# Sparse attention and an MLP on one core: regrouping the TensorE runs of batch 1, and two products less in batch 0

## The chip, the core and the metric

The kernel runs on one core of a Trainium2 chip. The metric is the device time of one execution in microseconds. A core has TensorE (PE in the profile, with its weight loads as PEld), VectorE (DVE), ScalarE (ACT), GpSimd (POOL) and SyncE (SP, used here to issue DMAs). TensorE writes to PSUM; DVE and ACT read PSUM and write SBUF.

## The reference, cut to what matters

```
B, H, S, D = 8, 8, 576, 64
scores = q @ k^T / sqrt(D)
local mask   (heads 0-3): 0 <= i - j < 32
strided mask (heads 4-7): i >= j and j % 32 == i % 32
attn = softmax(where(mask, scores, -1e9)) @ v          # per head
x    = attn, heads side by side                        # 4608 tokens x 512
h    = x @ w_in                                        # 512 -> 2048
g    = h * tanh(softplus(h))                           # Mish
out  = g @ w_out                                       # 2048 -> 512
```

## The kernel before, in words

Only the scores that a mask lets through are computed. The local heads are cut into 6 tiles of 96 queries, two head pairs each (12 units); the strided heads into 16 units of 72 queries. Each kind has three parts: the strided kind's parts 0, 1 and 2 hold 6, 6 and 4 units, the local kind's 5, 5 and 2. The third parts are what the change calls the third scores.

An attention step is one of these, all written out in program order by hand (`tc.manual_schedule()`), so that each engine's order is the order of the code:

- `t_str` and `t_loc` transpose q or k by PE into a PSUM tile. A call is for one pair of heads (`hp`); `t_loc` makes 12 transposes of 96 columns and returns the eviction, which the caller gives to DVE or ACT. `qTl` and `kTl` are the results for the local heads.
- `qk` (short `Q`) computes the scores of one or more parts in one run of matmuls (line 310), and ACT's exponentials (line 320 or 324) follow, one for each part.
- `mask` (`M`) multiplies by the mask on DVE (line 330).
- `pv` (`V`) multiplies the probabilities by v for one tile of queries (4 matmuls, line 346) into a small PSUM tile, and DVE normalises: a reciprocal (357) and a multiplication (358). `pv2` does two neighbouring tiles into one accumulator, with one reciprocal (371) and one multiplication (372) for both.
- `xt` and `xt_now` (`X`) transpose the result for the MLP; `xt_later` does so by DMA.

PSUM has small tiles of one bank, `tile_t`, of which two exist and are handed out in turn, and accumulators of two banks, `acc(0)` to `acc(2)`. A new use of a tile waits until what the last use left in it has been read.

The MLP goes by blocks of 512 tokens. While block t is computed, the attention of batch t+1 is threaded in. Block 0 differs from the others: its second product (`mlp2`, line 802) has 16 groups of four 512-column matmuls, and after group i the steps `at[i]` of batch 1 are issued. Their list is returned by `attn_steps` in the case `x == y`, where the one accumulator that attention has is `acc(x)`, with x = 0. The other blocks use another list, which the change leaves as it is. Some loads and sums of the weights hang on the same step numbers: `sums_w` on steps 0, 7, 9 and 11, loads for batch 2 on step 3 (issued by POOL), the transposing DMAs of batch 2 on step 12 (issued by SP), `sums_x` on step 14.

Batch 0 is computed ahead of the blocks, with nothing beside it. Between its steps stand products of a tile of zeros that nothing reads, `unread(n, i_acc)` (line 258): n matmuls of 512 columns into a small tile or into the first half of an accumulator. The call at line 931 is `unread(2, 2)`, between the transposes of the strided q (lines 929 and 930) and the bias matmuls of the third strided part (line 932), which write the same accumulator.

Of the kernel before, what the change touches and what calls it, by code (L numbers as in the profile page):

```python
# [11 lines left out]
BF16 = mybir.dt.bfloat16  # L12
# [31 lines left out]
def kernel(ctx, tc, q, k, v, moe_w_in, moe_w_out, out):  # L44
    nc = tc.nc
# [60 lines left out]
    def acc(i, name):  # L106

        pool = ps_z[0] if i == 2 else ps_a
        return pool.tile([128, 2, 512], F32, tag=f"acc{i}", name=name)
# [10 lines left out]
    def tile_t(name):  # L120
        return ps_t.tile([128, 512], F32, tag="pt", name=name)
# [11 lines left out]
    def by_head(x):  # L133

        return x[0:PL].rearrange("p j h d -> p (j h d)").rearrange("p (h x) -> p h x", h=4)
# [19 lines left out]
    def spread_v_str(b, eng):  # L155
        cast(eng, vs[b % 2][0:PN, :, :, 0:D], vs_raw().rearrange("p h (j d) -> p h j d", d=D))
# [23 lines left out]
    def cast(eng, out_, in_):  # L180
        if eng is nc.scalar:
            nc.scalar.copy(out_, in_)  # L182
        else:
            eng.tensor_copy(out_, in_)
# [35 lines left out]
    def t_loc(b, which, hp, tr):  # L220
        src = by_head((ql if which == "q" else kl)[b % 2])
        for j in range(CL):
            for e in range(2):
                nc.tensor.transpose(
                    tr[64 * e:64 * e + 64, PL * j:PL * j + PL],
                    src[:, 2 * hp + e, D * j:D * j + D], ident[0:PL, 0:PL],
                )
        dst = qTl[:, hp, :] if which == "q" else kTl[:, hp, 32:32 + S]
        return lambda eng: cast(
            eng, dst.rearrange("c (p j) -> c p j", j=CL),  # L230
            tr[:, 0:S].rearrange("c (j p) -> c p j", j=CL),
        )

    def t_str(b, which, hp, tr):
        src = (qs if which == "q" else ks)[b % 2]
        for u in range(8):
            h, jj = 2 * hp + u // 4, u % 4
            nc.tensor.transpose(  # L238
                tr[:, PN * u:PN * u + PN], src[0:PN, h, 128 * jj:128 * jj + 128],
                ident[0:PN, 0:PN],  # L240
            )
        dst = (qTs if which == "q" else kTs)[:, 8 * SU * hp:8 * SU * hp + 8 * SU]
        return lambda eng: cast(
            eng, dst.rearrange("c (u n) -> c u n", u=8)[:, :, 0:PN],
            tr[:, 0:S].rearrange("c (u n) -> c u n", u=8),
        )

    def t_step(b, kind, which, hp, eng=None):

        eng = eng or nc.vector  # L250
        tr = tile_t("tr")[:].bitcast(BF16)
        (t_str if kind == "s" else t_loc)(b, which, hp, tr)(eng)

    def unread(n, i_acc=None):

        tr = tile_t("un")[:] if i_acc is None else acc(i_acc, "un")[:, 0, :]
        for _ in range(n):
            nc.tensor.matmul(tr, lhsT=zeros[:, 0:128], rhs=zeros, start=True, stop=True)  # L258
# [165 lines left out]
    def attn_steps(b, x, y):  # L424

        a = Attn(b)
        Q = lambda i_acc, *parts: (lambda: a.qk(parts, i_acc))
        M = lambda kd, i: (lambda: a.mask(kd, i, nc.vector))
        V = lambda kd, i: (lambda: a.pv(kd, i))
        X = lambda kd, hf: (lambda: a.xt(kd, hf))  # L430
        s0, s1, sl2, l0, l1 = ("s", 0), ("s", 1), (("s", 2), ("l", 2)), ("l", 0), ("l", 1)
        if x == y:
            T = [(lambda n=n: t_step(b, *T_ORDER[n])) for n in (2, 3)]

            def t_first():
                tr = acc(x, "tr")
                copies = [t_str(b, w, 0, tr[:, n, :].bitcast(BF16)) for n, w in enumerate("kq")]
                for copy in copies:
                    copy(nc.vector)

            def t_pair(which):
                tr = acc(x, "tr")
                copies = [t_loc(b, which, hp, tr[:, hp, :].bitcast(BF16)) for hp in range(2)]
                for copy, eng in zip(copies, (nc.vector, nc.scalar)):
                    copy(eng)

            return [
                T,
                [Q(x, s0), Q("t", s1), lambda: spread_v_str(b, nc.vector), M(*s0), M(*s1)],
                [],  # L450
                [V("s", 0)],
                [V("s", 1), Q(x, ("s", 2))],
                [V("s", 2), M("s", 2), lambda: t_pair("k")],
                [V("s", 3)],
                [V("s", 4), lambda: t_pair("q")],
                [V("s", 5)],
                [V("s", 6), Q(x, l0)],
                [V("s", 7), M(*l0), Q(x, l1)],
                [X("s", 0), V("l", 0), M(*l1), Q(x, ("l", 2))],
                [X("s", 1), V("l", 1), M("l", 2)],  # L460
                [V("l", 2), V("l", 3)],
                [V("l", 4), V("l", 5)],
                [lambda: a.xt_now(5, nc.vector), lambda: a.xt_later(5)],
            ], [t_first]
        V2 = lambda kd, i, z: (lambda: a.pv2(kd, i, z))
        G = lambda kd, i: (lambda: a.mask(kd, i, nc.gpsimd))
        l2 = ("l", 2)
        now = -(-(512 * (b + 1) - S * b) // WQ)
        at = [
            [],  # L470
            [Q(x, s0), Q(y, s1), Q("t", *sl2), M(*s0), M(*s1), M("s", 2)],
            [],
            [V2("s", 0, y), G(*l2)],
            [],
            [V2("s", 2, y), Q(x, l0), Q("t", l1), G(*l0), G(*l1)],
            [],
            [V2("s", 4, y), lambda: nc.scalar.preload_act_table(AF.Mish)],
            [],
            [V2("s", 6, y)],
            [V2("l", 0, x)],  # L480
            [X("s", 0), V2("l", 2, y), X("s", 1)],
            [V2("l", 4, x), lambda: a.xt_now(now)],
            [lambda: a.xt_later(now)],
        ]
        return at
# [395 lines left out]
    with tc.manual_schedule():  # L881
# [39 lines left out]
        a = Attn(0)  # L921
# [6 lines left out]
        unread(5, 2)  # L928
        t_step(0, "s", "q", 0, Sc)
        t_step(0, "s", "q", 1, Dv)  # L930
        unread(2, 2)
        ps.append(a.bias("s", 2, 2))
        for i in range(2):
            a.qk([("s", i)], None, ps[i])
# [44 lines left out]
        for t in range(NBLK):  # L979
            if t == 0:  # L980
                x, y, z = accs
                at, ts = attn_steps(1, y, y)
                at[3] += [
                    lambda: load_early_v_str(2), lambda: load_tiles_loc(2, kl, k, (0, 1)),
# [13 lines left out]
            else:  # L998
                if t == 1:
                    split_third()  # L1000
                x, y = 0, 1
                gT, z, g1 = mlp1(t, (y, x) if t == 1 else (x, y))
                at = attn_steps(t + 1, x, y) if t + 1 < B else []
                if t == 1:
                    at[0].append(lambda: sums_w()[3](hi))
# [63 lines left out]
```

## Time and profile before

| | us |
|---|---|
| median of 3 runs (lowest, highest) | 285.5 (285.01, 285.75) |
| the profiled execution | 285.73 |
| its span on the core | 284.0 |
| PE busy | 277.0 |
| DVE busy | 199.1 |
| ACT busy | 197.3 |
| POOL busy | 109.6 |

The span runs from the first to the last instruction; the 1.7 us beside it in the execution's time lie around it. Busy times are sums over the span and can overlap between engines. Batch 0's attention fills about the first 22 us, the first product of block 0 the time to 34 us, the second product with the steps of batch 1 the stretch from 34 to 56 us; from there on one block follows another.

### The profile page before, as it was taken

How to read it: one execution, taken by the hardware profiler on the slowest of the kernel's cores; microseconds unless marked ns; L12 is line 12 of the kernel's file. 1: busy time of each engine (PE TensorE's matmuls, PEld its weight loads, DVE VectorE, ACT ScalarE, POOL GpSimd, SP SyncE). 2: the span in 40 equal slices, each digit the busy share in tenths (PEclk: the TensorE clock that was granted, in tenths of full speed). 3: DMA queues.
4: the chain of work that ended last, by engine and by line, in shares of the span. 5: the costliest groups of instructions: out<-in, count | busy, mean ns of one | idle time of the engine just before them, and what ended most of it. 6: DMA issues, size and time to landing. Idle time of an engine off the chain costs nothing.

```text
span 284.0 us, 7580 instructions
## 1 busy us (share of the span) xinstructions
PE 277.0 (98%) x3128; PEld 220.7 (78%) x3143; DVE 199.1 (70%) x415; ACT 197.3 (69%) x296; POOL 109.6 (39%) x129
## 2 busy tenths in 40 slices
PE   8999999999999999999999999999999999999994
PEld 2565755686898689868988898789878997888683
DVE  4176778889786778778767778777877767644742
ACT  1578663699857985798679877987798769417820
POOL 8584457307380729071907173625432500000000
PEclk9999999999999999999999999999999999999999
DMA  8999999999997999699969998999979041003004
GB/s 148 186 206 203 190 168 165 145 175 220 147 159 126 219 174 163 113 217 156 174 115 214 158 151 140 212 129 179 131 210 71 3 162 24 0 30 120 2 0 148
DMA packets 102685, 40.14 MB, mean 141 GB/s; under 512 B 85116, under 2 KB 98156, under 8 KB 102652
## 3 DMA queue, kind: packets, MB, share of 16 engines
q0 software_dynamic: 37728, 15.12, 50.6%
q1 hardware_dynamic: 64636, 24.31, 48.7%
q8 instruction: 24, 0.39, 0.6%
q10 hardware_dynamic: 288, 0.25, 0.3%
q14 instruction: 9, 0.07, 0.1%
HBM read 36.82 MB, written 9.44 MB: 163 GB/s over the span
## 4 chain that ended last, share of the span: by engine, by line
PE 86%; DMA 7%; DVE 2%; ACT 2%; SPq 1%; issue 1%; POOL 0%; DVEq 0%; POOLq 0%
PE pso L769 26%; PE psu L535 10%; PE psb L535 9%; PE psv L535 8%; PE psh L512 7%; DMA ql<-in_q_dram 6%; PE pso L829 4%; PE psb L512 4%; PE pso L802 4%; PE po L346 4%; PE un L258 3%; PE ps L310 3%; DMA kTl<-kl 1%; PE trx L395 1%; PE tr L238 1%; ACT Pl L324 1%
## 5 line engine op out<-in xcount | busy, mean ns | idle before, releaser
L535 PEld LDWEIGHTS <-w_in 128*128 128x128 bf16 x416 | 40.5, 98 | 9.2 <-issue 0.3
L769 PEld LDWEIGHTS <-gT 128*128 128x128 bf16 x448 | 41.9, 98 | 5.8
L330 POOL TENSOR_TENSOR Pl<-Pl,consts_sb 128x960 bf16<-128x960 bf16 (+1 forms) x18 | 29.2, 1636 | 43.3 <-issue 30.2
L769 PE MATMUL pso<-w_out,gT 128*128 128x256 bf16 x336 | 40.9, 272 | 0.0
L769 PEld LDWEIGHTS <-Sg 128*128 128x128 bf16 x336 | 31.5, 98 | 4.4
L535 PEld LDWEIGHTS <-Sw 128*128 128x128 bf16 x312 | 30.5, 98 | 4.0
L182 ACT COPY xT<-trx 128x576 bf16<-128x576 bf16 (+3 forms) x24 | 14.2, 629 | 18.5 <-PE trx L395 12.8
L512 PEld LDWEIGHTS <-w_in 128*128 128x128 bf16 x176 | 17.1, 98 | 12.6 <-issue 0.5
L769 PE MATMUL pso<-Tw,Sg 128*128 128x256 bf16 x224 | 26.7, 273 | 0.0
L544 ACT ACTIVATE gT<-psu 128x1024 bf16<-128x1024 f32 x18 | 18.5, 1025 | 9.9 <-PE psu L535 9.9
L160 POOL DMA_DIRECT2D vl<-in_v_dram x30 | 22.6, 760 | 6.9 <-DMA w_out<-in_moe_w_out_dram 2.6
L182 ACT COPY osb<-pso 128x512 f32<-128x512 f32 (+1 forms) x17 | 9.4, 555 | 20.2 <-PE pso L769 10.8
L512 PE MATMUL psh<-xT,w_in 128*128 128x512 bf16 (+1 forms) x95 | 22.2, 361 | 0.6
L675 DVE TENSOR_TENSOR psu<-psb,p 128x512 f32<-128x512 f32 x18 | 12.6, 700 | 14.5 <-PE psb L535 13.5
L372 DVE TENSOR_TENSOR x_s<-po,rden 72x512 bf16<-72x512 f32 x28 | 19.2, 687 | 1.0
L535 PE MATMUL psb<-Sx,w_in 128*128 128x256 bf16 x144 | 19.4, 272 | 0.0
L535 PE MATMUL psu<-xT,w_in 128*128 128x256 bf16 x136 | 18.9, 272 | 0.2 <-ACT psb L560 0.2
L675 DVE TENSOR_TENSOR Sg<-gT 128x256 bf16<-128x256 bf16 (+2 forms) x32 | 12.8, 422 | 8.0 <-ACT gT L544 6.7
L647 POOL COPY mark<-qTl 1x4 bf16<-1x4 bf16 x6 | 2.0, 334 | 42.4 <-DMA qTl<-ql 34.1
L746 DVE TENSOR_TENSOR p<-pso,p 128x512 f32<-128x512 f32 x14 | 9.6, 685 | 11.8 <-PE pso L769 11.8
L512 PE MATMUL psb<-xT,w_in 128*128 128x512 bf16 (+1 forms) x72 | 16.4, 355 | 0.0
L802 PE MATMUL pso<-w_out,gT 128*128 128x512 bf16 x59 | 15.8, 380 | 0.4 <-issue 0.2
(141 smaller groups left out, 617.5 us busy)
## 6 DMA issues: line engine op xcount, KB each, us to landing
out_dram<-osb SPq DMA_DIRECT2D x9, 512.0 KB, 3.9
out_dram<-p SPq DMA_DIRECT2D x7, 512.0 KB, 3.0
kl<-in_k_dram SPq DMA_DIRECT2D x5, 576.0 KB, 13.8
ql<-in_q_dram SPq DMA_DIRECT2D x5, 576.0 KB, 16.3
qs<-in_q_dram POOLq DMA_DIRECT2D x8, 288.0 KB, 12.3
vsr<-in_v_dram POOLq DMA_DIRECT2D x8, 288.0 KB, 9.8
vl<-in_v_dram POOLq DMA_DIRECT2D x30, 72.0 KB, 4.8
w_in<-in_moe_w_in_dram POOLq DMA_DIRECT2D x4, 512.0 KB, 12.1
```

The lines of the kernel that those rows point to most:

```text
L160: nc.gpsimd.dma_start(vl[b % 2][32:128, :, h, 0:D], v[b, h].rearrange("(w p) d -> p w d", p=WQ))
L182: nc.scalar.copy(out_, in_)
L330: meng.tensor_tensor(out=pm, in0=pm, in1=mk[0:n, :].unsqueeze(1).unsqueeze(1).to_broadcast([n, 2, nu, w]), op=ALU.mult,)
L346: nc.tensor.matmul(po[:, h, :], lhsT=pt[0:n, c0:c0 + 128], rhs=rhs, start=True, stop=True,)
L372: nc.vector.tensor_tensor(out=dst.rearrange("p e (h d) -> p e h d", h=4), in0=po[0:m, :, :, 0:D], in1=rden[0:m].unsqueeze(3).to_broadcast( ...
L512: nc.tensor.matmul(ps_u[:, o:o + n], lhsT=w_in[:, cc, fc * 128:(fc + 1) * 128], rhs=xT[:, cc, a:a + n], start=(cc == 2 and (o == 0 or len( ...
L535: nc.tensor.matmul(p[:, 256 * j:256 * j + 256], lhsT=lhs[:, cc, f:f + 128], rhs=rhs[:, cc], start=(first and j == 0 and cc == 0), stop=(la ...
L544: nc.scalar.activation(gT[:, c:c + src.shape[1], 256 * half_t:256 * half_t + 256], src, AF.Mish,)
L675: nc.vector.tensor_tensor(out=out_, in0=in0, in1=in1, op=op)
L769: nc.tensor.matmul(ps[:, pair, :], lhsT=lhs(c, 128 * pair), rhs=rhs(c), start=(first and pair == 0 and c == 0), stop=(last and c == 7), sk ...
L802: nc.tensor.matmul(p[:, ot % 2, :], lhsT=gT[:, fc, 128 * ot:128 * ot + 128], rhs=w_out[:, fc, :], start=(fc == 0), stop=(fc == 15),)
L829: nc.tensor.matmul(ps[n][:, 0:256], lhsT=lhs(c, 128 * n), rhs=rhs(c), start=(first and c == 0), stop=(last and c == 7), skip_group_check=True,
```

## The change: what it does

In the list of batch 1's steps:

- The local q and k, which were transposed in two runs of 24 (k in step 5, q in step 7, both into the accumulator), are transposed in one run of 48 in step 5: q into the two small tiles, k into the accumulator. ACT evicts the first half of q and of k, DVE the second halves.
- The third strided scores (step 4) and the third local scores (step 11) are computed in one run in step 7, with the two exponentials behind it. The strided mask that follows goes from step 5 to step 8; the local one stays in step 12.
- The strided products 1 and 2 (steps 4 and 5) become one `pv2` in step 4, the local products 2 and 3 (step 13) one `pv2` in the same step, both in the accumulator.

In batch 0 the call `unread(2, 2)` goes.

```diff
-            def t_pair(which):
+            def t_local():
+                copies = [t_loc(b, "q", hp, tile_t("tr")[:].bitcast(BF16)) for hp in range(2)]
                 tr = acc(x, "tr")
-                copies = [t_loc(b, which, hp, tr[:, hp, :].bitcast(BF16)) for hp in range(2)]
-                for copy, eng in zip(copies, (nc.vector, nc.scalar)):
+                copies += [t_loc(b, "k", hp, tr[:, hp, :].bitcast(BF16)) for hp in range(2)]
+                for copy, eng in zip(copies, (nc.scalar, nc.vector) * 2):
                     copy(eng)
 
             return [
...
                 [V("s", 0)],
-                [V("s", 1), Q(x, ("s", 2))],
-                [V("s", 2), M("s", 2), lambda: t_pair("k")],
+                [lambda: a.pv2("s", 1, x)],
+                [t_local],
                 [V("s", 3)],
-                [V("s", 4), lambda: t_pair("q")],
-                [V("s", 5)],
+                [V("s", 4), Q(x, *sl2)],
+                [M("s", 2), V("s", 5)],
                 [V("s", 6), Q(x, l0)],
                 [V("s", 7), M(*l0), Q(x, l1)],
-                [X("s", 0), V("l", 0), M(*l1), Q(x, ("l", 2))],
+                [X("s", 0), V("l", 0), M(*l1)],
                 [X("s", 1), V("l", 1), M("l", 2)],
-                [V("l", 2), V("l", 3)],
+                [lambda: a.pv2("l", 2, x)],
                 [V("l", 4), V("l", 5)],
...
         t_step(0, "s", "q", 1, Dv)
-        unread(2, 2)
         ps.append(a.bias("s", 2, 2))
```

## The prediction

> **What bounds the kernel now.** I read the page first (busy shares, slices, the chain's sum), then the waits of PE, then the timeline of the two stretches that the change touches. The columns of a timeline row are start, length, engine, line, operation, tiles and count, and in brackets the idle time before it with what ended it.
>
> ```profile
> PE 277.0 (98%) x3128; PEld 220.7 (78%) x3143; DVE 199.1 (70%) x415; ACT 197.3 (69%) x296; POOL 109.6 (39%) x129
> ...
> PEclk9999999999999999999999999999999999999999
> ...
> PE 86%; DMA 7%; DVE 2%; ACT 2%; SPq 1%; issue 1%; POOL 0%; DVEq 0%; POOLq 0%
> ```
>
> ```profile
> PE ps L281 <- PE tr L238: 0.3, 1, 0.3
> PE po L346 <- DVE x_s L372: 0.2, 1, 0.2
> ```
>
> PE is busy for 277.0 of 284.0 us, and apart from its start no wait of it is recorded as longer than 0.3 us; the two shown are those in batch 0. So PE's own stream is the bound, and what leaves that stream, or shortens a stall hidden inside it, should show at the end one for one. Busy lengths overlap, since matmuls are pipelined; I therefore price a run by the distance from its start to the start of the next run.
>
> **Batch 0: the two products (line 931).**
>
> ```profile
> 1.20 6.58 PE L258 MATMUL un<-Tw 128*128 128x512 bf16 x16 [1.20 <-DVE Tw L896]
> ...
> 10.61 0.68 PE L238 MATMUL tr<-consts_sb,qs 72*128 72x72 bf16 x16
> 11.13 0.38 PE L258 MATMUL un<-Tw 128*128 128x512 bf16 x1
> 11.78 0.40 PE L281 MATMUL ps<-consts_sb 72*128 72x288 bf16 x2 [0.27 <-PE tr L238]
> 12.12 0.56 PE L310 MATMUL ps<-qTs,kTs 64*128 64x72 bf16 x24
> ...
> 13.37 0.70 PE L224 MATMUL tr<-consts_sb,kl 96*64 96x96 bf16 x24
> ```
>
> ```profile
> 11.07 0.64 ACT L182 COPY qTs<-tr 128x576 bf16<-128x576 bf16 x1 [1.43 <-PE tr L238]
> ```
>
> ```profile
> 11.33 0.46 DVE L184 COPY qTs<-tr 128x576 bf16<-128x576 bf16 x1 [5.46 <-PE tr L238]
> ```
>
> One of the two products has a record (11.13). The bias matmuls behind them write the same accumulator and start at 11.78, when the products are through. Without them the bias can start at 11.13 and takes 0.34 (11.78 to 12.12). The score run behind it then waits for the evictions of the strided q: ACT's ends at 11.07 + 0.64 = 11.71, DVE's at 11.33 + 0.46 = 11.79. The score run starts at about 11.82 in place of 12.12: a gain of 0.30 us. Its bounds are 0.43 (two products at 0.217, the spacing of the 512-column products: 4 in 0.87 below) and nothing (the evictions or a load hold the rest). The next load needed is the local k of batch 0:
>
> ```profile
> 3.65 0.69 POOL L146 DMA_DIRECT2D kl<-in_k_dram  x1
> ...
> 35.01 0.76 POOL L175 DMA_DIRECT2D w_out<-in_moe_w_out_dram  x1 [1.14 <-DMA w_out<-in_moe_w_out_dram]
> ```
>
> ```profile
> kl<-in_k_dram POOLq DMA_DIRECT2D x1, 288.0 KB, 9.1
> ```
>
> ```profile
> w_out<-in_moe_w_out_dram POOLq DMA_DIRECT2D x1, 512.0 KB, 13.1
> ```
>
> It lands at 3.65 + 9.1 = 12.75, and its transposes move from 13.37 to 13.07: still 0.3 behind it. The ACT and DVE work that follows in batch 0 hangs on these runs and moves with them.
>
> **Batch 1: the new order.** "Step n" is what follows the nth group of four 512-column products (line 802), counted from 0. The rows touched:
>
> ```profile
> 40.52 0.29 PE L346 MATMUL po<-vs,Ps 72*128 72x65 bf16 x4
> 40.74 0.30 PE L310 MATMUL ps<-qTs,kTs 64*128 64x72 bf16 x8
> 40.98 1.04 PE L802 MATMUL pso<-w_out,gT 128*128 128x512 bf16 x4
> ...
> 44.56 0.29 PE L346 MATMUL po<-vs,Ps 72*128 72x65 bf16 x4
> 44.78 0.70 PE L224 MATMUL tr<-consts_sb,Sg 96*64 96x96 bf16 x24
> 45.41 1.04 PE L802 MATMUL pso<-w_out,gT 128*128 128x512 bf16 x4
> ...
> 50.39 0.29 PE L346 MATMUL po<-vl,Pl 128*128 128x65 bf16 x4
> 50.62 0.26 PE L310 MATMUL ps<-qTl,kTl 64*128 64x96 bf16 x4
> 50.81 1.04 PE L802 MATMUL pso<-w_out,gT 128*128 128x512 bf16 x3
> ...
> 52.94 0.50 PE L346 MATMUL po<-vl,Pl 128*128 128x65 bf16 x8
> 53.28 1.02 PE L802 MATMUL pso<-w_out,gT 128*128 128x512 bf16 x4
> 54.14 0.66 PE L346 MATMUL po<-vl,Pl 128*128 128x65 bf16 x8
> 54.64 1.02 PE L802 MATMUL pso<-w_out,gT 128*128 128x512 bf16 x4
> ...
> 73.00 0.41 PE L346 MATMUL po<-vs,Ps 72*128 72x65 bf16 x8
> 73.24 1.91 PE L769 MATMUL pso<-Tw,Sg 128*128 128x256 bf16 x16
> ```
>
> Group 13 gives the product's price: 53.28 to 54.14, 0.86 to 0.87 for four. A pair of probability products alone (8 matmuls, 73.00) takes 0.24, so a single one 0.12; followed by a score or transpose run of half-height or half-width operands it takes 0.22 (40.52, 44.56). Going into such a run thus costs 0.10, and by the same comparison coming out of it about 0.10 (eight 72-column score matmuls in 0.24, while two runs back to back grow by much less). Step by step:
>
> - Step 4: one product and eight scores, 40.52 to 40.98, 0.46. After: one pair, 0.24. Gain 0.22.
> - Steps 5 and 7: each one product and 24 transposes, 44.56 to 45.41, 0.85; together 1.70. After, step 5 has 48 transposes alone: 0.10 going in, and twice 0.63 less what one exit saves, 1.16 to 1.26. I take 1.24 with the entry (bounds 1.16, no entry cost, and 1.36). Step 7 has one product (0.22) and 12 scores: 0.24 + 0.19 (rows 40.74 and 50.62) less one exit, 0.33 (bounds 0.33 and 0.43), so 0.55. Loss of the two steps: 1.24 + 0.55 = 1.79, that is 0.09 more.
> - Step 11: product and four scores, 50.39 to 50.81, 0.42; after 0.13. Gain 0.29.
> - Step 13: 0.34 now, though a free pair takes 0.24. Step 14: 0.50. The chain of waits says why:
>
> ```profile
> 54.02 0.43 DVE x_l L358
> ...
> 54.50 0.30 PE po L346 x4
> ```
>
> PE's second product of step 14 starts only when DVE has emptied the tile two products earlier. The pair of step 13 now goes to the accumulator, not to the two small tiles, so step 14 finds its tiles emptied since step 12. Gain 0.10 + 0.26 = 0.36; nothing if DVE, which has the same masks and sums to do, holds PE elsewhere.
>
> Sum in batch 1: 0.22 - 0.09 + 0.29 + 0.36 = 0.78, bounds 0.78 - 0.12 - 0.10 - 0.36 = 0.20 and 0.86.
>
> What is hidden, and by what margin. The 48 transposes use both small tiles (q) and the accumulator (k). DVE must empty the new pair from that accumulator first:
>
> ```profile
> 14.93 0.69 DVE L372 TENSOR_TENSOR x_s<-po,rden 72x512 bf16<-72x512 f32 x1
> ...
> 42.73 0.45 DVE L330 TENSOR_TENSOR Ps<-Ps,consts_sb 72x576 bf16<-72x576 bf16 x1
> ...
> 46.20 0.96 DVE L675 TENSOR_TENSOR Tw<-w_out 128x1024 bf16<-128x1024 bf16 x1
> ```
>
> ```profile
> 43.88 0.64 ACT L182 COPY kTl<-tr 128x576 bf16<-128x576 bf16 x1 [2.14 <-DVE kTl L184]
> ```
>
> The pair ends on PE near 40.46; reciprocal and multiply take some 0.9, to 41.5; k's transposes come after a product group (0.87) and q's 24, near 41.95. Margin 0.4. The four evictions are shared: ACT one q and one k (2 x 0.64), DVE the others; the ACT row shows that two copies into one tensor run one after the other, so DVE's k copy waits for ACT's, to about 43.8. The local scores of step 7 come near 44.5. The third strided mask is now behind a weight sum on DVE (0.96 at worst, then 0.45): done near 46.55, and the product that reads it comes near 46.7: margin 0.15, the thinnest. The local scores moved out of step 11 leave ACT and DVE less to do in steps 11 to 13. Loads: the last quarter of w_out lands at 35.01 + 13.1 = 48.1; step 12 now starts near 49.9. The DMA that overwrites the strided k transposed, and with it SP's queue, had to wait for the third strided scores (40.98 now, about 44.8 after), but it goes out well behind either:
>
> ```profile
> 50.69 1.45 SPq L209 DMA_TRANSPOSE kTs<-ks  x1
> ```
>
> Total 0.30 + 0.78 = 1.08, bounds 0.2 and 1.3. The profiled execution took 285.73 us (span 284.0), so 284.65 for such an execution; against the median of 285.5, 284.4 us.
>
> **The rivals.**
>
> New waits eat it: the third strided mask late by up to 0.5, or the pair's emptying late for k's transposes by up to 0.4, so that 0.4 to 0.7 of 1.08 is left: 284.8 to 285.1, say 284.9. For it, the 0.15 margin and that DVE already held PE in step 14; against it, that DVE has two instructions less at two places.
>
> Hidden anyway: the loads, not PE, pace batches 2 to 5, and waits there take back what was won: 285.4. For it, loads that take 9 to 13 us to land (above); against it, PE shows no DMA wait at all in the waits above.
>
> Slower: the clock. The first 16 products at 1.20 took 0.40 each against 0.217 later, so PE started at about half rate, though the PEclk row shows 9 throughout; only the spacing tells it. If the stretch from 10.6 to 14 without the two products falls back to that rate for 3 to 6 us, it loses 1.5 to 3 us less what DVE and ACT bound there anyway, some 2 us: 286.4. It decides from 1.1 us on. Against it: the stretch from 14 to 20 has no such product at all today, 24 transposes and a 0.2 us wait, and then
>
> ```profile
> 22.27 4.32 PE psh L512 x20
> ```
>
> runs at 0.216. The Trainium skill ("TensorE: Matmul & The Clock Gate", PE-mode transpose) says that transposes don't count as PE-busy for this gate in the same way, which speaks against removing the products amid transposes; by its window of about 3.4 us at half rate, an estimate, the loss would be up to 1.7 us. No run so far shows a fall back.
>
> **How the numbers follow.** My forecast 0.62; new waits 0.22; hidden anyway 0.07; clock 0.09. A measurement of this kernel tells about 0.3% (0.86 us) from no change. Of my forecast's 0.62 some 0.07 ends under 0.86; of the new waits 0.05 still end above it. Faster 0.60, same 0.31, slower 0.09. The range goes down to 283.8 (gain 1.3 and the runs' own spread of some 0.4 below the median) and up to 285.6 (gain 0.2 and 0.3 of spread).
>
> **What would show it.** Right: the score run of batch 0 near 11.8; 48 transposes in one row of about 1.2 us; steps 13 and 14 at 0.24 each; the group of products at 54.64 near 53.6; everything later moved by the same. Wrong: PE idle ahead of the 48 transposes' second half, ahead of step 9's product, or products spaced 0.4 after 11 us; or a shift at 54 us that is not there at the end.

## The result, and the profile after

The changed kernel takes 284.13 us in the median of 7 runs (283.97 to 284.55), the kernel before beside it 285.26 us (284.68 to 285.75). The ratio is 0.9962, with a 95% interval of 0.995 to 0.9974: 0.7 to 1.4 us faster. The profiled execution took 284.2 us, with a span of 282.4 us, against 285.73 and 284.0 before.

Busy shares and the chain's sum of the page after, then the longest waits of PE behind its first one:

```profile
PE 275.0 (97%) x3126; PEld 219.2 (78%) x3141; DVE 200.6 (71%) x411; ACT 197.2 (70%) x296; POOL 110.8 (39%) x129
...
PE 91%; DMA 3%; DVE 1%; POOL 1%; ACT 1%; issue 1%; POOLq 0%
```

```profile
PE po L346 <- DVE Ps L330: 0.5, 1, 0.5
PE pso L803 <- issue: 0.3, 2, 0.2
PE ps L281 <- DVE x_s L372: 0.3, 1, 0.3
PE ps L310 <- ACT qTs L182: 0.2, 1, 0.2
```

PE still bounds the kernel. But its longest wait is new: a product (line 346) waits 0.5 us for a mask (line 330). The timeline of PE shows it, with the steps that changed:

```profile
1.20 5.38 PE L258 MATMUL un<-Tw 128*128 128x512 bf16 x16 [1.20 <-DVE Tw L897]
...
9.71 0.69 PE L238 MATMUL tr<-consts_sb,qs 72*128 72x72 bf16 x16
10.24 0.41 PE L281 MATMUL ps<-consts_sb 72*128 72x288 bf16 x2
10.87 0.59 PE L310 MATMUL ps<-qTs,kTs 64*128 64x72 bf16 x24 [0.22 <-ACT qTs L182]
...
39.33 0.41 PE L346 MATMUL po<-vs,Ps 72*128 72x65 bf16 x8
39.58 1.03 PE L803 MATMUL pso<-w_out,gT 128*128 128x512 bf16 x4
40.53 1.21 PE L224 MATMUL tr<-consts_sb,Sg 96*64 96x96 bf16 x48
...
43.54 0.29 PE L346 MATMUL po<-vs,Ps 72*128 72x65 bf16 x4
43.76 0.30 PE L310 MATMUL ps<-qTs,kTs 64*128 64x72 bf16 x8
43.90 0.25 PE L310 MATMUL ps<-qTl,kTl 64*128 64x96 bf16 x4
44.08 1.04 PE L803 MATMUL pso<-w_out,gT 128*128 128x512 bf16 x4
...
45.07 1.03 PE L803 MATMUL pso<-w_out,gT 128*128 128x512 bf16 x4
46.57 0.30 PE L346 MATMUL po<-vs,Ps 72*128 72x65 bf16 x4 [0.47 <-DVE Ps L330]
...
51.96 0.42 PE L346 MATMUL po<-vl,Pl 128*128 128x65 bf16 x8
52.22 1.02 PE L803 MATMUL pso<-w_out,gT 128*128 128x512 bf16 x4
53.08 0.42 PE L346 MATMUL po<-vl,Pl 128*128 128x65 bf16 x8
53.34 1.02 PE L803 MATMUL pso<-w_out,gT 128*128 128x512 bf16 x4
```

The group of four products that starts at 45.07 takes 0.87 and ends at 45.94; the product of step 9 starts at 46.57, so 0.63 us are lost there. Everywhere else the new order is as short as the prediction's prices: step 4 takes 0.25, step 7 0.54, steps 13 and 14 0.26 each. What held the mask stands on DVE and POOL:

```profile
44.42 0.68 DVE L676 TENSOR_TENSOR Tw<-w_out 128x1024 bf16<-128x1024 bf16 x1
45.01 1.50 DVE L330 TENSOR_TENSOR Ps<-Ps,consts_sb 72x576 bf16<-72x576 bf16 x1
```

```profile
44.80 1.40 POOL L184 COPY vl<-vl 32x1280 bf16<-32x1280 bf16 x1 [0.33 <-DMA vl<-in_v_dram]
```

The mask takes 1.50 us where it took 0.45 before. It starts while POOL copies the shared v rows (`share_v_loc(1, Po)` in step 3's list, which waits until those rows have been loaded) and ends 0.31 us after that copy's end. In the kernel before, the same copy began ahead of the weight sum at 46.20 that took 0.96:

```profile
45.36 1.25 POOL L184 COPY vl<-vl 32x1280 bf16<-32x1280 bf16 x1 [0.38 <-DMA vl<-in_v_dram]
```

Beside this, the two profiled executions differ in something that the change does not touch: the transposes behind the first 16 products (which start at 1.20) begin at 7.62 before and at 6.42 after. Among the profiled executions of this study the first transposes start between 5.95 and 7.62. So single executions must not be subtracted from each other as a whole. I use two distances inside an execution:

- the start: from the transposes of the strided q to the score run, 10.61 to 12.12 before (1.51 us), 9.71 to 10.87 after (1.16);
- batch 1: from the first 512-column group (line 802 or 803) to the first product of the next block, 34.88 to 55.93 before (21.05 us), 33.69 to 54.63 after (20.94).

The start gained 0.35 us, batch 1 only 0.11. The one other stretch from the score run on that differs by more than 0.1 us gained 0.25 us; it is shown with the experiments.

### The profile page after: what moved, and what is told of

The parts are those of the page before. It is cut to its first block, busy times and chain, and to the rows that moved or that the text cites. A ratio compares the mean times of both kernels' runs of the same rounds, so it can differ in the third digit from the quotient of the medians.

```text
span 282.4 us, 7573 instructions
## 1 busy us (share of the span) xinstructions
PE 275.0 (97%) x3126; PEld 219.2 (78%) x3141; DVE 200.6 (71%) x411; ACT 197.2 (70%) x296; POOL 110.8 (39%) x129
## 4 chain that ended last, share of the span: by engine, by line
PE 91%; DMA 3%; DVE 1%; POOL 1%; ACT 1%; issue 1%; POOLq 0%
PE pso L770 31%; PE psu L536 11%; PE psb L536 9%; PE psv L536 9%; PE psh L513 7%; PE psb L513 5%; PE po L346 4%; PE pso L830 4%; PE pso L803 4%; DMA ql<-in_q_dram 3%; PE ps L310 3%; PE trx L395 1%; PE tr L224 1%; PE trx L410 1%; DVE Ps L330 1%
## 5 line engine op out<-in xcount | busy, mean ns | idle before, releaser
L372 DVE TENSOR_TENSOR x_s<-po,rden 72x512 bf16<-72x512 f32 x29 | 19.9, 687 | 1.0
L330 DVE TENSOR_TENSOR Ps<-Ps,consts_sb 72x864 bf16<-72x864 bf16 (+1 forms) x21 | 12.6, 604 | 5.0 <-ACT Ps L324 4.8
```

Source lines behind the costliest of these rows:

```text
L330: meng.tensor_tensor(out=pm, in0=pm, in1=mk[0:n, :].unsqueeze(1).unsqueeze(1).to_broadcast([n, 2, nu, w]), op=ALU.mult,)
L372: nc.vector.tensor_tensor(out=dst.rearrange("p e (h d) -> p e h d", h=4), in0=po[0:m, :, :, 0:D], in1=rden[0:m].unsqueeze(3).to_broadcast( ...
```

## The experiments

Times are ratios to the kernel before, run beside each kernel. "Start" and "batch 1" are the two distances just named. With four products and with POOL's copy later, batch 1 holds 0.11 and 0.18 us of another delay: the first strided product comes 4.75 and 4.82 us after the first group, 4.64 in all other kernels. A DVE copy of v rows (line 184) ahead of the first masks took 1.52 and 1.59 us there, 0.69 to 1.41 elsewhere; the cause was not tested.

| kernel | ratio (95% interval) | start, us | batch 1, us |
|---|---|---|---|
| before | 1 | 1.51 | 21.05 |
| changed | 0.9962 (0.995 to 0.9974) | 1.16 | 20.94 |
| changed, a second time | 0.9977 (0.9965 to 0.9989) | 1.15 | 20.94 |
| two products less, old order | 0.9992 (0.9984 to 1.0001) | 1.15 | 21.06 |
| new order, products kept | 0.9968 (0.9957 to 0.9979) | 1.51 | 20.93 |
| four products, old order | 1.0011 (1.0001 to 1.0021) | 1.94 | 21.17 |
| changed, ACT copies the rows | 0.9943 (0.9931 to 0.9955) | 1.15 | 20.29 |
| changed, POOL copies later | 0.996 (0.9945 to 0.9976) | 1.16 | 20.46 |
| changed, POOL copies twice | 0.9967 (0.9955 to 0.9979) | 1.16 | 21.41 |

### The two parts apart

The kernel before with only the products removed:

```diff
-        unread(2, 2)
         ps.append(a.bias("s", 2, 2))
```

> The kernel before, with only the two unread products taken out of batch 0; batch 1 in its old order. Theory A (the prediction's own term): 0.3 us faster than before, because the score run then waits for the evictions of q. Rival B (the products are worth more, since everything behind them in batch 0 hangs on them, and batch 1's new order gives little because its third strided mask came late): 0.6 to 1.1 us faster. Rival C (the loads hold the start anyway): no difference.

The changed kernel with the products put back:

```diff
         t_step(0, "s", "q", 1, Dv)
+        unread(2, 2)
         ps.append(a.bias("s", 2, 2))
```

> The changed kernel with the two unread products put back in batch 0; batch 1 in its new order. Theory A as predicted: 0.8 us faster than before. Rival B, from the profile after, in which product 6 waited for the third strided mask (0.5 to 0.6 us): 0.1 to 0.3 us faster only. In the profile the mask's length tells: 1.50 us again if it meets POOL's copy of the shared v rows, 0.45 if not.

The kernel before with four products:

```diff
-        unread(2, 2)
+        unread(4, 2)
```

> The kernel before, with four unread products of 512 columns at the place where it has two. Theory A: two products on PE's path cost 0.43 us, so 0.43 us slower than before. Rival C (start-up loads give slack): less than 0.2 us slower. If the clock at the start matters (more products keep it up or bring it up sooner): no slower, or faster.

PE's timeline of the first of these, around the place:

```profile
10.59 0.69 PE L238 MATMUL tr<-consts_sb,qs 72*128 72x72 bf16 x16
11.11 0.41 PE L281 MATMUL ps<-consts_sb 72*128 72x288 bf16 x2
11.74 0.58 PE L310 MATMUL ps<-qTs,kTs 64*128 64x72 bf16 x24 [0.22 <-ACT qTs L182]
```

The bias follows the transposes at once and the score run waits 0.22 us for the eviction, as predicted. The start shortens by 0.36, and two products more lengthen it by 0.43, which is their whole length. The measured times agree: 0.0 to 0.5 us faster, where no change lies just inside the interval, and 0.0 to 0.6 us slower. The traces settle the first part, the times do not contradict them.

The new order alone has the collision too: its mask again takes 1.50 us, and batch 1 is 0.12 shorter. Its time, 0.6 to 1.2 us below that of before, is more than that. Part of the rest is a place that I had not expected. In the block that starts near 142 us ACT's first copy starts 0.62 us after its last instruction before, 0.34 after:

```profile
144.44 1.06 ACT L560 COPY psb<-psu 128x512 f32<-128x512 f32 x2 [0.62 <-PE psu L535]
```

```profile
142.87 1.06 ACT L561 COPY psb<-psu 128x512 f32<-128x512 f32 x2 [0.34 <-PE psu L536]
```

With it the block takes 29.22 us before and 28.97 after (first product to first product of the next block: 143.04 to 172.25, and 141.74 to 170.72). The 0.62 is there in all three kernels with the old order, the 0.34 in all others. So the new order is worth 0.12 + 0.25 = 0.37 us in the traces. Why ACT was late at that instruction, and what more there is in the time of this one kernel, stays open. The differing start of the executions is one candidate that these runs cannot separate: the first transposes begin between 6.86 and 7.62 in the three profiled executions of the old order, between 5.95 and 7.61 in the others.

### What held the mask

The copy of the shared rows goes from POOL to ACT, behind the exponentials of the third scores:

```diff
-                    lambda: share_v_loc(1, Po), lambda: load_tiles_loc(2, kl, k, (2, 3)),
+                    lambda: load_tiles_loc(2, kl, k, (2, 3)),
...
+                at[8].append(lambda: share_v_loc(1))
```

> The changed kernel, with the copy of the shared v rows of batch 1 (line 166) made by ACT in step 8 and no longer by POOL in step 3's list. If POOL's copy is what held the mask on DVE: the mask takes 0.45 us in place of 1.50, PE's wait of 0.5 us ahead of product 6 goes, and the kernel is 0.5 to 0.6 us faster than the changed one. If the mask was late for another reason (ACT's exponentials, the weight sum ahead of it): its length stays over 1 us and the time is that of the changed kernel. If ACT becomes the bound in step 9 instead (1.3 us of copy ahead of the local exponentials): PE waits ahead of the local scores of step 10 and the gain is 0.2 or less.

DVE's, ACT's and PE's rows of it:

```profile
44.93 0.68 DVE L676 TENSOR_TENSOR Tw<-w_out 128x1024 bf16<-128x1024 bf16 x1
45.53 0.45 DVE L330 TENSOR_TENSOR Ps<-Ps,consts_sb 72x576 bf16<-72x576 bf16 x1
```

```profile
45.74 1.26 ACT L182 COPY vl<-vl 32x1280 bf16<-32x1280 bf16 x1
```

```profile
45.58 1.03 PE L803 MATMUL pso<-w_out,gT 128*128 128x512 bf16 x4
46.45 0.29 PE L346 MATMUL po<-vs,Ps 72*128 72x65 bf16 x4
```

The mask stands in the same place behind the same weight sum, and takes 0.45 us. The product follows its group at once. PE does not wait ahead of the local scores of step 10. Batch 1 shrinks from 20.94 to 20.29 us, 0.76 below the kernel before, and the time is 1.3 to 2.0 us below it. This version is faster than both kernels: its five runs took 283.37 to 283.87 us, the fourteen of the changed kernel 283.97 to 285.10. Some 0.16 us of the difference to the changed kernel is not the mask's, since the last block is shorter too (see the end).

The copy later on POOL:

```diff
-                    lambda: share_v_loc(1, Po), lambda: load_tiles_loc(2, kl, k, (2, 3)),
+                    lambda: load_tiles_loc(2, kl, k, (2, 3)), lambda: share_v_loc(1, Po),
```

> The changed kernel, with POOL's copy of the shared v rows put behind the second pair of the k loads, where it starts near 47.5 in place of 44.8. If DVE's operations on bf16 pairs are held while POOL copies (theory): the strided mask takes 0.45 us and PE has no wait at product 6, and what DVE does near 47.5 to 49 (a weight sum of 0.68, or the first local mask of 0.65) is stretched by up to 1.2 us in its place; the kernel then is between 0.5 us faster than the changed one and as fast, by whether the first local product comes late. If the mask was long for a reason of its own (its place behind the weight sum): it stays at 1.50 and nothing near 48 is stretched.

```profile
45.42 0.45 DVE L330 TENSOR_TENSOR Ps<-Ps,consts_sb 72x576 bf16<-72x576 bf16 x1
```

```profile
45.68 1.30 POOL L184 COPY vl<-vl 32x1280 bf16<-32x1280 bf16 x1
```

The copy started at 45.68 and not near 47.5, since the loads ahead of it went out sooner than I thought. The mask came first and took 0.45; nothing was stretched in its place, against my expectation. Until the copy ends at 46.98 DVE has only reciprocals and normalisations, which read PSUM; its next operation on two bf16 tensors starts at 47.22. Without the 0.18 us of the other delay, batch 1 would be as short as with ACT's copy. The time cannot be told from the changed kernel's.

The copy made twice:

```diff
-                    lambda: share_v_loc(1, Po), lambda: load_tiles_loc(2, kl, k, (2, 3)),
+                    lambda: share_v_loc(1, Po), lambda: share_v_loc(1, Po), lambda: load_tiles_loc(2, kl, k, (2, 3)),
```

> The changed kernel with POOL's copy of the shared rows made twice, one right behind the other. If POOL's copy holds DVE's mask: the mask, where it starts during a copy, takes about 1.2 us longer than with one copy (up to 2.7), PE waits some 1.7 us at product 6, and the kernel is 0.7 to 1.3 us slower than the changed one; if DVE gets in between two copies, it ends after the first. If the length of 1.50 had another cause: the mask stays at 1.50 or 0.45 and the time that of the changed kernel to 0.3 us.

DVE, POOL and PE:

```profile
44.70 1.16 DVE L676 TENSOR_TENSOR Tw<-w_out 128x1024 bf16<-128x1024 bf16 x1
45.78 1.50 DVE L330 TENSOR_TENSOR Ps<-Ps,consts_sb 72x576 bf16<-72x576 bf16 x1
```

```profile
44.06 2.90 POOL L184 COPY vl<-vl 32x1280 bf16<-32x1280 bf16 x2
```

```profile
47.33 0.29 PE L346 MATMUL po<-vs,Ps 72*128 72x65 bf16 x4 [0.95 <-DVE Ps L330]
```

Here the two engines take turns. The first copy holds the weight sum (1.16 for 0.68), the weight sum ends, the second copy runs, then the mask. So the second copy does not hold the mask longer; it holds the sum ahead of it, and PE waits 0.95 in place of 0.47. In batch 1's length the second copy costs 0.47 us. The time, which I expected 0.7 to 1.3 us above the changed kernel's, is not clear of it: the ratio lies between the two ratios of that kernel. Part of the cost is hidden by the last block, which is 0.18 us shorter here than in the changed kernel. Only the trace shows the cost.

The changed kernel a second time:

> The changed kernel as it is, in another execution. What is open: by its first profile the new order saves 0.12 us of block 0's length (25.04 for 25.16), by the times 0.7 to 0.9. If the collision of the strided mask with POOL's copy depends on when the v rows land: the mask takes 0.45 to 1.50 us by where POOL's copy lies, and block 0 is between 24.4 and 25.04 long. If every execution has the collision: 1.50 and 25.04 again.

The 25.04 and 25.16 us count block 0 from an earlier product, at 29.59 and 30.77; in the distance used here they are 20.94 and 21.05. Its copy and DVE's two operations:

```profile
44.42 2.09 POOL L184 COPY vl<-vl 32x1280 bf16<-32x1280 bf16 x1 [0.43 <-DMA vl<-in_v_dram]
```

```profile
44.73 0.68 DVE L676 TENSOR_TENSOR Tw<-w_out 128x1024 bf16<-128x1024 bf16 x1
45.32 1.50 DVE L330 TENSOR_TENSOR Ps<-Ps,consts_sb 72x576 bf16<-72x576 bf16 x1
```

The copy starts 0.38 us earlier than in the first execution, and the mask takes 1.50 us all the same: this time the copy is the longer one, 2.09 us, because the weight sum runs through its middle at full speed. In all four executions in which a copy was under way when the sum ended, the copy went first and ended 1.11 us after the sum, and the mask waited for it. That is why batch 1 is 20.94 both times, and 20.93 with the products kept. I had expected a length that depends on when the v rows land; for copies that start between 0.31 us ahead of the sum and 0.39 us behind its start it does not. Why the sum was not held in this execution, though the copy had started 0.31 us ahead of it, is not shown; with the copy made twice, where the lead was 0.64 us, it was held.

The Trainium skill ("GPSIMD Engine Reference", Specifications) says that GpSimd shares its SBUF interfaces with VectorE and that DVE instructions with two SBUF inputs contend with it. The runs agree, and show the size: up to 1.05 us for one mask of 0.45.

### The other terms of the new order

These start from the version in which ACT copies the rows, so that the collision is away. Its batch 1 takes 20.29 us.

| from that version | ratio (95% interval) | batch 1, us |
|---|---|---|
| local pair apart | 0.9961 (0.9949 to 0.9973) | 20.91 |
| third scores apart | 0.9956 (0.9944 to 0.9968) | 20.50 |
| transposes in two runs | 0.9969 (0.996 to 0.9979) | 21.02 |
| strided pair apart | 0.9972 (0.996 to 0.9983) | 20.84 |
| two more products less, ahead of q | 0.9942 (0.993 to 0.9955) | 20.29 |

The local products 2 and 3 apart:

```diff
-                [lambda: a.pv2("l", 2, x)],
+                [V("l", 2), V("l", 3)],
```

> The changed kernel with the shared rows copied by ACT (the run before), and the local products 2 and 3 each normalised on its own in the small tiles, as in the kernel before. By the prediction's term for steps 13 and 14: 0.36 us slower than the run before, the run of 8 matmuls at step 14 taking 0.50 again and that of step 13 0.34. Rival: the stall at step 14 came from DVE's mask of the third local part in step 12, which is free of its wait now, so less than 0.15 us slower.

```profile
52.14 0.29 PE L346 MATMUL po<-vl,Pl 128*128 128x65 bf16 x4
52.64 0.30 PE L346 MATMUL po<-vl,Pl 128*128 128x65 bf16 x4 [0.21 <-DVE x_l L358]
52.78 1.02 PE L803 MATMUL pso<-w_out,gT 128*128 128x512 bf16 x4
53.64 0.66 PE L346 MATMUL po<-vl,Pl 128*128 128x65 bf16 x8
54.14 1.02 PE L803 MATMUL pso<-w_out,gT 128*128 128x512 bf16 x4
```

Step 13 takes 0.64 and step 14 0.50, for 0.26 each. The pair is worth 0.62 us, more than the 0.36 of the sum, because PE now comes to step 13 earlier and DVE hardly does: counted from the first group, PE's first product there starts at 17.62 us (18.06 before), DVE's emptying of the tile that the second one needs at 17.64 (17.78 before).

The third scores apart:

```diff
-                [V("s", 4), Q(x, *sl2)],
+                [V("s", 4), Q(x, ("s", 2))],
...
-                [X("s", 0), V("l", 0), M(*l1)],
+                [X("s", 0), V("l", 0), M(*l1), Q(x, ("l", 2))],
```

> The changed kernel with the shared rows copied by ACT, and the third local scores back in step 11, alone. By the prediction's terms: step 11 takes 0.29 us more, step 7 0.09 us less, so 0.20 us slower than the changed kernel with ACT's copy. Rival: the exponential of 0.48 us moved back into step 11 delays ACT's copy of the transposed strided result and with it more, 0.4 us slower or beyond.

Batch 1 is 0.21 longer, the sum's 0.20.

The local transposes in two runs (`t_pair("q")` uses the small tiles, `t_pair("k")` the accumulator):

```diff
-                [t_local],
-                [V("s", 3)],
+                [lambda: t_pair("q")],
+                [V("s", 3), lambda: t_pair("k")],
```

> The changed kernel with the shared rows copied by ACT, and the local transposes in two runs of 24, q in step 5 and k in step 6. By the price of going into and coming out of such a run (0.10 each): 0.1 to 0.2 us slower than with one run. Rival: no cost of its own for a run, so within 0.05 us in the block's length; k's evictions come one group later, and if the scores of step 7 wait for them, 0.3 us slower or more.

```profile
44.59 0.31 PE L310 MATMUL ps<-qTs,kTs 64*128 64x72 bf16 x8 [0.43 <-DVE kTl L184]
```

The rival holds here: k's evictions come too late for the scores of step 7, PE waits 0.43, and batch 1 is 0.73 longer. Of this, 0.50 lies between the product of step 7 and the scores (0.72 for 0.22). The rest is the price of a second run, as the prediction had it: the two runs of 24 take 0.63 each, the one of 48 takes 1.15, and the product ahead of the second run 0.22 in place of 0.12, together 0.21 us more.

The strided products 1 and 2 apart:

```diff
-                [lambda: a.pv2("s", 1, x)],
-                [t_local],
+                [V("s", 1)],
+                [V("s", 2), t_local],
```

> The changed kernel with the shared rows copied by ACT, and the strided products 1 and 2 again each normalised on its own, in step 4 and in step 5 ahead of the 48 transposes. By the prices of the prediction (0.12 + 0.22 for 0.24 + 0.10): block 0 as long as with the pair, within 0.05 us. Rival: the transposes of q need the small tiles that these products use, and wait for DVE to empty the second one: 0.3 to 0.6 us longer.

```profile
41.84 0.96 PE L224 MATMUL tr<-consts_sb,Sg 96*64 96x96 bf16 x36 [0.35 <-DVE x_s L358]
```

Again the rival: the transposes stop after 12, because the second small tile has not been emptied. Batch 1 is 0.55 us longer.

The start with fewer products, ahead of the transposes of the strided q:

```diff
-        unread(5, 2)
+        unread(3, 2)
```

> The changed kernel with the shared rows copied by ACT, and three unread products in place of five ahead of the transposes of the strided q. If PE's products still pace the start: up to 0.43 us faster than with five. If the load of the strided q (landing near 9.7 to 10.0 us) paces it: no difference, and PE waits for that load. If fewer products let the clock fall: products spaced 0.43 after 8 us, and slower by 1 us or more.

```profile
PE tr L238 <- DMA qs<-in_q_dram: 0.5, 1, 0.5
```

No faster than with five: PE then waits for the load of the strided q. The start is held by loads from here on, and PE's rate did not fall: the three products take 0.81 us, and three in a row take 0.81 or 0.82 in the other kernels.

## Why the prediction was right, and where it was not

The prediction said 284.4 us and 1.08 us less than before; 284.13 and 1.13 were measured, and 0.3 to 1.0 us less when the kernel was run a second time. The sum came out, its terms did not all, and that it came out so closely is partly luck. In the two profiled executions the change is worth 0.35 us at the start, 0.11 in batch 1 and 0.25 at a place that the prediction did not have: 0.71 us. The rest of the 1.13 lies in no stretch of these traces that the change touches; the changed kernel's second measurement, 0.77 us below the kernel before in the medians, lies close to the 0.71.

- Batch 0, 0.30 us: right in mechanism and size. The start shortened by 0.35 to 0.36, the score run waits for q's eviction, and the time of this part alone is 0.23 us lower (-0.03 to 0.46).
- Batch 1, 0.78 us: the prices of the steps were right as prices. With POOL's copy moved to ACT, batch 1 is 0.76 us shorter. In the changed kernel itself it is 0.11.
- The step that failed is the margin of the third strided mask: "behind a weight sum on DVE (0.96 at worst, then 0.45)", done near 46.55, with 0.15 us to spare. It was the thinnest margin, and its rival, a late mask at up to 0.5 us, was named at 0.22; the wait was 0.47 us, and 0.63 us of the step's length. PE idle ahead of step 9's product was also one of the prediction's own signs of being wrong. What was missed lies beside the row quoted there. The weight sum of 0.96 before was 0.68 long elsewhere; POOL's copy (45.36 to 46.61) lay beside its beginning at 46.20. I took the 0.96 as an upper bound for that sum and the mask's 0.45 as fixed, but the 0.96 was the sign of a partner that would hold whichever of DVE's two-tensor operations came next.
- The 0.25 us near 142 us made up for part of the loss. It stood in no term; without it the time would have been nearer to the rival's 284.9.
- The margin of 0.4 us for k's transposes held: 48 transposes in one row of 1.21, with no wait inside. It hangs on the pair: with its two products apart the transposes stop for 0.35.
- Hidden anyway: not so for batches 2 to 5, whose blocks are as long as before but for the one near 142 us. At the start it is near, and in part true. The margin of 0.3 us for the local k was used up in some executions whose first transposes came early: with ACT's copy and with two copies on POOL, where they begin at 5.95 and 6.44, PE waits 0.21 and 0.26 us for that load, out of the 0.35 that the start gains. Two products fewer still (five to three) gain nothing, because the load of the strided q holds the start.
- The clock: PE kept its rate behind the score run without the two products (the unread products there take 0.82 us before and after), and with another two less ahead of q. The fall that the Trainium skill's sentence on transposes allows ("TensorE: Matmul & The Clock Gate", PE-mode transpose) did not show in any run here. What varies is when the rate rises at first: the first transposes start between 5.95 and 7.62 us with the same 16 products. In the kernel before, the first fourteen intervals between these are 0.43 us each, with ACT's copy the first six; the others are 0.22 to 0.27.

## What to carry to other kernels

An operation that now and then takes 1.4 times its usual time on an engine can be a trace of something that it shares; before it is used as a bound, look up what runs beside it, here a POOL copy beside a DVE operation on two SBUF tensors. A margin of 0.15 us on a path that goes through a shared interface is no margin: the collision took 0.65 of the 0.76 us that the reordering is worth, and moving the copy to ACT, which had room for it, gave them back. And when executions differ by up to 1.7 us in their start alone, compare stretches inside an execution; in the two profiled executions of the changed kernel the two distances used here repeated to 0.02 us.

## What was not expected of the hardware

- A POOL copy (32x1280 bf16, 1.25 us alone) and a DVE operation on two bf16 SBUF tensors did not run side by side here: the one that was held ended as long after the other as it takes alone, less some 0.13 us. That is 0.31 us for the mask of 0.45, 0.55 for the weight sum of 0.68, 1.11 for the copy. So the mask took 1.50 us in each of four executions in which a copy was waiting, and the weight sum 1.16 when a copy was ahead of it. An overlap of 0.14 us cost nothing: with two products only, the weight sum starts that long before the copy's end and keeps its 0.68. The recorded starts do not tell which goes first: a copy that had started 0.31 us ahead of the sum took 2.09 us, with the sum at full speed in its middle. DVE's reciprocals and normalisations out of PSUM kept their 0.17 and 0.42 beside a copy.
- The last block is about 0.16 us shorter in most of the kernels derived from the changed one (28.86 for 29.02, as in the version with ACT's copy), but not in the changed kernel; nothing here explains it.
